# Writing down TensorE's order between attention and the gate, and exchanging two Strassen products

## The chip, the cores and the metric

One core of a Trainium2 chip runs the whole program. The metric is device microseconds of one execution; beside it stands one profiled execution, from which all rows come. TensorE multiplies matrices (its rows are marked PE, its weight loads PEld), VectorE (DVE) and ScalarE (ACT) do elementwise work and empty the accumulation banks (PSUM), GpSimd (POOL) does elementwise work on SBUF alone, and SyncE (SP) issues DMAs.

## The reference

Three stages in float32, with batch 2, 8 heads, 576 positions and head size 64, so 1152 tokens of 512 features:

```python
x = softmax_attention(mean4(q), mean4(k), mean4(v)) repeated 4x + band_attention(q, k, v)
logits = x @ w_gate                      # 512 x 8
P = exp(logits - max); 8 x: P /= rowsum; P /= colsum; P *= N / E
y = sum over 8 experts of P[:, e] * (relu(x @ w1[e]) @ w2[e])      # 512 -> 1024 -> 512
out = softplus(y @ w_in) @ w_out         # 512 -> 2048 -> 512
```

## The kernel before

**Precision.** Every float32 operand of a large product is split into a high part that TensorE takes exactly and a remainder: xh and xl for tokens, w1h and w1l for weights. A product is three matmuls (high x high, low x high, high x low) for each block of 128 rows.

**Seven products for eight.** The first layer of each expert, and of the last MLP, is computed by a Strassen-like scheme over 2 x 2 blocks: seven products (numbers 0 to 6), each of six matmuls (`product`, L589 to L601), of precomputed sums of blocks of weights and tokens (`ORDER` says in which order the tokens' seven operands are made, `operands` makes them). The tokens come in two passes, s = 0 with column halves of 256 and four tiles of 128 tokens, and s = 1 with halves of 320 and five tiles. One call of `first(n)` is step n: seven products, with a `yield` behind each. Product 4 goes into one bank of the pool m, which ScalarE copies out (t1); product 0 into a second (copied out as t5); product 5 into a third, from which VectorE makes the sum c11 = m5 + t1. Product 2 adds itself to the first bank, and ScalarE copies the sum out as u2. Product 3 adds itself to the second bank, and VectorE makes c12 = that + u2. Product 1 adds itself to the first bank, and VectorE makes c22 = that + t5. Product 6 adds itself to the first bank, which is then the fourth result. A matmul that writes a bank waits until the bank's last reader has finished. Each result goes through `hidden`: for an expert a ReLU on ScalarE (hh) and a remainder on VectorE (hl); for the last MLP a longer chain of Abs, Exp, Ln and sums.

**Second layer.** `second(n, ...)` is the share of step n in one token tile's output: six matmuls of 512 columns into a bank yps. When a group of steps is complete, `weigh` adds the bank to the accumulator on VectorE.

**Order.** Where nothing else is said, a planner decides at build time in which order each engine gets its instructions, from its own estimate of the times, earlier traced work first. Inside `tc.manual_schedule(engines={PE})` TensorE's instructions stay in the order in which the code traces them; the other engines' order is still the planner's. Before the change only the main loop (L781 on, from step 4) is written down so. There, the shares of step n, one for each token tile, are dealt among the seven products of step n + 2: with four tiles the pattern is two products, share, two, share, two, share, one, share; with five it is two, share, two, share, one, share, one, share, one, share.

**Beside attention.** Attention runs first, eight units of heads, in blocks of scores, transpositions (`turn`) and values. From half of it on, the first four steps (expert 0, first pass) are traced among its blocks by the generator `beside`: its 44 items are 4 x 7 products and 16 shares. The shares of two steps make one token tile's output, in one bank, y, which `weigh` empties before the next tile. After attention's loop the rest of `beside` is traced, then attention's buffers are given up, the second pass's operands are made in their place, then come the gate (`gates`: for each pass two groups of eight matmuls lt with 16 outputs, copied out by ScalarE as lts, and a fold by small matmuls into lg) and steps 4 and 5. TensorE's order in all this is the planner's. Then the main loop begins; it also contains the gate's normalisation (`sinkhorn`) and 32 pieces of a conversion of the last MLP's weights (`convert`, tiles cva), mostly on VectorE and GpSimd.

The banks: pool m has three, pool at has four (attention's, later the outputs'), and y is one.

Of the kernel before, what the change touches and what calls it, by code (L numbers as in the profile page):

```python
# [19 lines left out]
def attention_moe_mlp(ctx: ExitStack, tc: tile.TileContext, q, k, v, w_gate, w1, w2, w_in, w_out, out):  # L20
    nc = tc.nc
    B, H, S, D = q.shape
    NT, DM = out.shape
    E, _, FF = w1.shape
    F2 = w_out.shape[0]
    P = 128
# [15 lines left out]
    HALF = (256, 320)  # L42
# [8 lines left out]
    OPS = 7  # L51
# [12 lines left out]
    def bank(tag, name):  # L64
        return ps.tile([P, 512], F32, tag=tag, bufs={"m": 3, "y": 1, "at": 4}[tag], name=name)

    def tmp(s, name):
        return tmpp.tile([P, HALF[1]], F32, tag="t", name=name)[:, : HALF[s]]

    def pair(name):  # L70
        return pairp.tile([P, 2, 2 * HALF[1]], F32, tag="pair", name=name)
# [165 lines left out]
            yield  # L237


    ORDER = (4, 0, 5, 1, 2, 6, 3)  # L240
    FASTI = (0, 1, 2, 6)

    def halves(s, x):
        return x[:, : HALF[s]], x[:, HALF[s] : 2 * HALF[s]]
# [215 lines left out]
    nc.scalar.copy(wgs[:, :, :, :E], wg)  # L460
    nc.vector.tensor_tensor(wgs[:, :, :, E:], wg, wgs[:, :, :, :E].bitcast(F32), op=ALU.subtract)

    def gates():
        lg = bank("y", "lg")
        for s in range(2):
            lts = pair("lts").rearrange("p a c -> p (a c)")[: 2 * E]
            for j in range(2):
                lt = bank("m", "lt")
                terms = [
                    (i, w, kk, x[s]) for i, w in (((4, 1), (5, 2)), ((3, 0), (1, 1)))[j]  # L470
                    for kk in range(2) for x in (xh, xl)
                ]
                for n, (i, w, kk, x) in enumerate(terms):
                    nc.tensor.matmul(
                        lt[: 2 * E, : HALF[s]], wgs[:, w, kk, :], x[:, i, kk, :],
                        start=(n == 0), stop=(n == len(terms) - 1),
                    )
                nc.scalar.copy(halves(s, lts)[j], lt[: 2 * E, : HALF[s]])
            for t in TILES[s]:
                o = t * P - T0[s]  # L480
                nc.tensor.matmul(lg[:, t * E : (t + 1) * E], lts[:, o : o + P], fold, start=True, stop=True)
        nc.vector.tensor_reduce(m1, lg[:, : NTT * E], axis=AX.X, op=ALU.max)
        nc.vector.tensor_copy(prf, lg[:, : NTT * E])

# [45 lines left out]
    BESIDE = 4  # L530
# [45 lines left out]
    def first(n):  # L576

        e, g, s, p = steps[n]
        h = HALF[s]
        wh, wl = weights[uses[n]][0]  # L580

        if n < turned[0] and n >= BESIDE + 2 and n % 3 == 0 or n >= turned[1] and (n - turned[1]) % 3 == 0:
            hh, hl = [pairp.tile([P, 4 * HALF[1]], F32R, tag="pair", name="h3") for _ in range(2)]
        else:
            hh = hp.tile([P, 4 * HALF[1]], F32R, tag="hh", name="hh")
            hl = hp.tile([P, 4 * HALF[1]], F32R, tag="hl", name="hl")
        hh, hl = [t[:, : 4 * h].rearrange("p (f c) -> p f c", f=2) for t in (hh, hl)]

        def product(i, b=None):  # L589
            more = b is not None  # L590
            if not more:
                b = bank("m", f"m{i}")
            n = 0
            for kk in range(2):
                for x, y in ((wh, xh), (wh, xl), (wl, xh)):
                    nc.tensor.matmul(  # L596
                        b[:, :h], x[:, i, kk, :], y[s][:, i, kk, :],
                        start=(not more and n == 0), stop=(n == 5), skip_group_check=more,
                    )
                    n += 1  # L600
            return b  # L601

        def kept(name, b):
            t = tmp(s, name)
            nc.scalar.copy(t, b[:, :h])  # L605
            return t

        def combine(name, b, t):
            c = tmp(s, name)
            nc.vector.tensor_tensor(c, b[:, :h], t, op=ALU.add)  # L610
            return c

        def emit(c, f, j):
            at_ = (f, slice(j * h, (j + 1) * h))
            hidden(e, s, c, hh, hl, at_)


        b1 = product(4)
        t1 = kept("t1", b1)
        yield  # L620
        b5 = product(0)
        t5 = kept("t5", b5)
        yield

        spare[0] = product(5)
        c11 = combine("c11", spare[0], t1)
        emit(c11, 0, 0)
        yield
        product(2, b1)
        u2 = kept("u2", b1)  # L630
        yield
        product(3, b5)
        c12 = combine("c12", b5, u2)
        emit(c12, 0, 1)
        yield
        product(1, b1)
        c22 = combine("c22", b1, t5)
        emit(c22, 1, 1)
        yield
        product(6, b1)  # L640
        emit(b1[:, :h] if e < E else kept("c21", b1), 1, 0)
        ready[n] = hh, hl
        yield
# [47 lines left out]
    def lead(n):  # L691
        yield from first(n)
        f = uses[n]
        if final[f] == n and f + 3 < len(fetches):
            fetch_first(f + 3, fetches[f + 3])
# [8 lines left out]
    def beside():  # L704

        for n0 in range(0, BESIDE, 2):
            e, g, s, p = steps[n0]
            for n in (n0, n0 + 1):
                for _ in lead(n):
                    yield 6 * HALF[s]  # L710
            for i in range(len(TILES[s])):
                y = bank("y", "yps")
                for n in (n0, n0 + 1):
                    second(n, *ready[n], i, y, n == n0, n == n0 + 1)
                    if n == n0:
                        yield 6 * DM
                weigh(e, s, i, y)
                yield 6 * DM
            used(n0)
            used(n0 + 1)  # L720
# [5 lines left out]
    units[1].load()  # L726
    LAG = 2
    DENSE = 3600
    side, columns = beside(), 0
    begin = len(stream) // 2 + LAG  # L730
    for n in range(len(stream) + LAG + 1):
        if n < len(stream):
            x, blk = stream[n]
            i, j = divmod(n, len(blocks))
            x.scores(blk)
            if j == 1 and 1 <= i <= 6:
                (fetch_first if i % 2 else fetch_second)((i - 1) // 2, (i - 1) // 2)
            if j >= 2 and i + 1 < len(units):
                for g in ((0, 1), (2,))[j - 2]:
                    units[i + 1].setup(g)  # L740
                if j == 3 and i + 2 < len(units):
                    units[i + 2].load()
        for lag, what in ((LAG, "turn"), (LAG + 1, "values")):
            if 0 <= n - lag < len(stream):
                x, blk = stream[n - lag]
                getattr(x, what)(blk)
        while columns < (n - begin) * DENSE:
            columns += next(side, 1 << 30)
    for _ in side:
        pass  # L750

    CV = 12
    PIECES = 2
    ready.clear()
    at.__exit__(None, None, None)
    operand_tiles(ctx.enter_context(tc.tile_pool(name="xp1", bufs=1)), 1)
    rows.append(ctx.enter_context(tc.tile_pool(name="rows1", bufs=len(TILES[1]))))
    for kk in range(2):
        for _ in operands(1, kk, Unit.pairs[1, kk], ORDER, [nc.gpsimd]):
            pass  # L760
    gates()
    for n in (BESIDE, BESIDE + 1):
        for _ in lead(n):
            pass


    ahead = {n: [n + 2] for n in range(BESIDE, len(steps) - 2)}
# [77 lines left out]
```

## Time and profile before

| | |
|---|---|
| median of 3 runs | 1136.76 us (1133.81 to 1138.63) |
| the profiled execution | 1142.66 us, span 1140.9 us |
| mean granted TensorE clock | 0.966 |
| busy: PE, PEld, DVE, ACT, POOL | 1077.5, 943.2, 781.3, 536.3, 498.8 us |

The span is the time from the first to the last instruction. A row of the timeline gives the start, the duration, the engine with line and operation, output tile and inputs, shapes and how many rows are merged; in brackets the idle time of the engine just before it and what ended it. Durations of matmuls overlap, as a matmul's end is modelled, and starts are the surer number. A granted clock of 1.00 is 2.4 GHz, and 0.50 is 1.2 GHz.

### The profile page before, as it was taken

The page shows a single profiled execution, that of the slowest core. Times are in us where ns is not written, and L with a number is a line of the kernel's source. Part 1 is how long each engine was busy: PE and PEld are TensorE (multiplying, and loading weights), DVE is VectorE, ACT ScalarE, POOL GpSimd, SP SyncE. Part 2 cuts the span into 40 slices and gives each one's busy share as a digit, 9 for nine tenths or more (in the row PEclk, how much of TensorE's full clock was granted, in tenths as well). Part 3 has the DMA queues.
Part 4 walks back from the last instruction along what each step waited for, and adds up shares of the span by engine and source line. Part 5 has one row for each costly group of instructions (what it writes and reads, how often), then busy time and mean ns, then how long its engine had stood idle before and what let it go on. Part 6 is the DMA issues. An engine that isn't in the chain of part 4 may idle for free.

```text
span 1140.9 us, 18021 instructions
## 1 busy us (share of the span) xinstructions
PE 1077.5 (94%) x6385; PEld 943.2 (83%) x6385; DVE 781.3 (68%) x1628; ACT 536.3 (47%) x1411; POOL 498.8 (44%) x537
## 2 busy tenths in 40 slices
PE   5799998999999999998999999999999998999998
PEld 4578877899988888887888888888887887888887
DVE  6969764764677675876668476776765657766665
ACT  4657743343343344433433343343442547767763
POOL 6724144463356565556655344343553301322321
PEclk8659998999999999999999999999999998999999
DMA  8533211211143434343433323222333255154112
GB/s 174 126 88 84 61 37 38 75 34 51 49 136 111 133 97 138 101 139 102 126 111 120 111 79 126 78 94 98 119 108 114 101 204 203 60 208 170 71 38 84
DMA packets 133498, 119.71 MB, mean 105 GB/s; under 512 B 35744, under 2 KB 111776, under 8 KB 133408
## 3 DMA queue, kind: packets, MB, share of 16 engines
q1 hardware_dynamic: 133408, 118.56, 33.5%
q8 instruction: 50, 0.82, 0.3%
q14 instruction: 40, 0.33, 0.1%
HBM read 93.11 MB, written 25.43 MB: 104 GB/s over the span
## 4 chain that ended last, share of the span: by engine, by line
PE 57%; DVE 21%; DMA 7%; POOL 6%; issue 5%; ACT 3%; SPq 1%; DVEq 0%; POOLq 0%; ACTq 0%
PE yps L655 26%; PE m L596 25%; DMA raw<-in_moe_w_out 2%; POOL sums L106 2%; DMA raw<-in_moe_w_in 2%; DVE c L610 2%; DVE acc L672 2%; DVE cva L173 2%; PE sc L361 1%; DVE xl L236 1%; DVE cva L174 1%; POOL w1l L134 1%; DVE raw L180 1%; DVE cva L177 1%; DVE cva L181 1%
## 5 line engine op out<-in xcount | busy, mean ns | idle before, releaser
L596 PE MATMUL m<-xh,w1h 128*128 128x320 f32 (+1 forms) x1120 | 340.9, 304 | 34.0 <-DVE c L610 22.9
L596 PE MATMUL m<-xl,w1h 128*128 128x320 f32 (+1 forms) x1120 | 334.1, 298 | 0.0
L596 PE MATMUL m<-xh,w1l 128*128 128x320 f32 (+1 forms) x1120 | 334.0, 298 | 0.0
L596 PEld LDWEIGHTS m<-xh,w1h 128*128 128x128 f32 x1120 | 213.7, 191 | 68.1 <-DVE c L610 37.7
L596 PEld LDWEIGHTS m<-xl,w1h 128*128 128x128 f32 x1120 | 213.9, 191 | 11.8 <-DVE qkd L321 0.4
L596 PEld LDWEIGHTS m<-xh,w1l 128*128 128x128 f32 x1120 | 213.8, 191 | 0.0
L655 PE MATMUL yps<-w2h,hh 128*128 128x512 f32 x520 | 207.5, 399 | 0.3 <-DVE acc L668 0.3
L655 PE MATMUL yps<-w2l,hh 128*128 128x512 f32 x520 | 206.7, 398 | 0.0
L655 PE MATMUL yps<-w2h,hl 128*128 128x512 f32 x520 | 204.4, 393 | 0.0
L149 POOL TENSOR_TENSOR w2l<-raw,w2h 128x512 fp32r<-128x512 f32 x72 | 97.3, 1370 | 125.1 <-ACT w2h L148 125.1
L557 ACT ACTIVATE hh<-c 128x256 fp32r<-128x256 f32 (+1 forms) x138 | 60.3, 444 | 183.9 <-DVE c L610 183.4
L655 PE MATMUL yps<-w2h,h 128*128 128x512 f32 x400 | 141.4, 394 | 0.0
L134 POOL TENSOR_TENSOR w1l<-sums,w1h 128x512 fp32r<-128x512 f32 x72 | 97.0, 1361 | 95.9 <-ACT w1h L133 58.9
L570 POOL TENSOR_TENSOR ab<-ab,up 128x320 f32<-128x320 f32 (+1 forms) x64 | 54.1, 845 | 162.6 <-ACT ln L566 121.7
L610 DVE TENSOR_TENSOR c<-m,t 128x256 f32<-128x256 f32 (+1 forms) x160 | 72.3, 452 | 68.4 <-PE m L596 67.1
L672 DVE SCALAR_TENSOR_TENSOR acc<-yps,pr,acc 128x512 f32<-128x512 f32 x117 | 87.1, 744 | 45.8 <-PE yps L655 43.0
L655 PEld LDWEIGHTS yps<-w2h,hl 128*128 128x128 f32 x520 | 98.7, 190 | 23.1 <-DVE hl L558 0.4
L655 PEld LDWEIGHTS yps<-w2h,hh 128*128 128x128 f32 x520 | 99.0, 190 | 14.1 <-DVE acc L668 0.6
L558 DVE SCALAR_TENSOR_TENSOR hl<-c,hh 128x256 fp32r<-128x256 f32 (+1 forms) x138 | 85.1, 620 | 35.0 <-ACT hh L557 33.7
L655 PEld LDWEIGHTS yps<-w2l,hh 128*128 128x128 f32 x520 | 99.1, 191 | 11.7
L655 PEld LDWEIGHTS yps<-w2h,h 128*128 128x128 f32 x400 | 75.7, 189 | 13.5
L605 ACT COPY t<-m 128x256 f32<-128x256 f32 (+1 forms) x160 | 62.5, 397 | 40.9 <-PE m L596 39.4
(136 smaller groups left out, 1675.3 us busy)
## 6 DMA issues: line engine op xcount, KB each, us to landing
raw<-in_moe_w SPq DMA_DIRECT2D x72, 256.0 KB
raw<-in_moe_w SPq DMA_DIRECT2D x36, 512.0 KB
w1h<-s_in SPq DMA_DIRECT2D x10, 896.0 KB
w1l<-s_in SPq DMA_DIRECT2D x10, 896.0 KB
raw<-in_moe_w_in SPq DMA_DIRECT2D x32, 256.0 KB
raw<-in_moe_w_out SPq DMA_DIRECT2D x16, 512.0 KB
w2l<-s_out SPq DMA_DIRECT2D x10, 512.0 KB
w2h<-s_out SPq DMA_DIRECT2D x10, 512.0 KB
```

The costliest lines, as they stand in the source:

```text
L106: nc.gpsimd.tensor_tensor(sums[i], a, b, op=op)
L134: nc.gpsimd.tensor_tensor(lo[:, part], sums, hi[:, part].bitcast(F32), op=ALU.subtract)
L149: nc.gpsimd.tensor_tensor(lo[:, i], raw[:, i], hi[:, i].bitcast(F32), op=ALU.subtract)
L173: nc.vector.tensor_scalar(a, high, 0x07FFFFFF, 3, op0=ALU.bitwise_and, op1=ALU.logical_shift_left)
L557: nc.scalar.activation(hh, c, AF.Relu)
L558: nc.vector.scalar_tensor_tensor(out=hl, in0=c, scalar=0.0, in1=hh.bitcast(F32), op0=ALU.max, op1=ALU.subtract)
L570: nc.gpsimd.tensor_tensor(ab, ab, up, op=ALU.subtract)
L596: nc.tensor.matmul(b[:, :h], x[:, i, kk, :], y[s][:, i, kk, :], start=(not more and n == 0), stop=(n == 5), skip_group_check=more,)
L605: nc.scalar.copy(t, b[:, :h])
L610: nc.vector.tensor_tensor(c, b[:, :h], t, op=ALU.add)
L655: nc.tensor.matmul(y, a[:, f, tok], b[:, f, :], start=(start and m == 0), stop=(stop and m == 5))
L672: nc.vector.scalar_tensor_tensor(out=acc[t], in0=y, scalar=pr[:, t, e : e + 1], in1=acc[t], op0=ALU.mult, op1=ALU.add,)
```

## The change

Products 1 and 3 change places in `first`, and operands 3 and 6 in `ORDER`. The gate becomes a generator in six parts, takes its banks from the pool at and its result tiles from the pool of temporaries, and keeps the two results of a pass in tiles of their own, so that one tile of the second pass is folded in two pieces. The rest of `beside` (14 items after the loop over attention), the gate's parts and the products of steps 4 and 5 are traced in a written-down order: six products of step 3 with the first pass's three gate parts between, four shares, then the 14 products of steps 4 and 5, with one item behind every second of them: three shares, three gate parts, one share.

```diff
-    ORDER = (4, 0, 5, 1, 2, 6, 3)
+    ORDER = (4, 0, 5, 1, 2, 3, 6)
...
-    def gates():
-        lg = bank("y", "lg")
+    def gates(banks):
+
+        lg = bank("at", "lg")
         for s in range(2):
-            lts = pair("lts").rearrange("p a c -> p (a c)")[: 2 * E]
+            lts = [tmp(1, "lts")[: 2 * E] for _ in range(2)]
             for j in range(2):
-                lt = bank("m", "lt")
+                if s or not j:
+                    whole = bank(banks, "lt")
+                lt = whole if s else halves(s, whole)[j]
...
-                nc.scalar.copy(halves(s, lts)[j], lt[: 2 * E, : HALF[s]])
+                nc.scalar.copy(lts[j][:, : HALF[s]], lt[: 2 * E, : HALF[s]])
+                yield
             for t in TILES[s]:
                 o = t * P - T0[s]
-                nc.tensor.matmul(lg[:, t * E : (t + 1) * E], lts[:, o : o + P], fold, start=True, stop=True)
+                for j in range(2):
+
+                    a, b = max(o, j * HALF[s]), min(o + P, (j + 1) * HALF[s])
+                    if a < b:
+                        nc.tensor.matmul(
+                            lg[a - o : b - o, t * E : (t + 1) * E], lts[j][:, a - j * HALF[s] : b - j * HALF[s]],
+                            fold, start=True, stop=True,
+                        )
+            yield
...
+        product(1, b1)
+        c22 = combine("c22", b1, t5)
+        emit(c22, 1, 1)
+        yield
         product(3, b5)
         c12 = combine("c12", b5, u2)
         emit(c12, 0, 1)
-        yield
-        product(1, b1)
-        c22 = combine("c22", b1, t5)
-        emit(c22, 1, 1)
         yield
         product(6, b1)
...
-    side, columns = beside(), 0
+    side, columns, shares = beside(), 0, BESIDE * (OPS + len(TILES[0]))
...
-            columns += next(side, 1 << 30)
-    for _ in side:
-        pass
+            columns += next(side)
+            shares -= 1
...
-    gates()
-    for n in (BESIDE, BESIDE + 1):
-        for _ in lead(n):
-            pass
+
+    gate = gates("at")
+    with tc.manual_schedule(engines={mybir.EngineType.PE}):
+        for n in range(shares - 4):
+            next(side)
+            if n in (1, 3, 5):
+                next(gate)
+        among = iter((side, side, side, gate, gate, gate, side))
+        for m, _ in enumerate(x for n in (BESIDE, BESIDE + 1) for x in lead(n)):
+            if m % 2:
+                next(next(among))
+        for x in (side, gate):
+            for _ in x:
+                pass
```

## Rows read from the trace of the kernel before

**Rows 1.** The page's first part: engine, busy us, share of span, instructions.
```profile
PE 1077.5 (94%) x6385; PEld 943.2 (83%) x6385; DVE 781.3 (68%) x1628; ACT 536.3 (47%) x1411; POOL 498.8 (44%) x537
```

**Rows 2.** TensorE's waits, 230 us to the end: us in total, times, longest.
```profile
PE m L596 <- DVE c L610: 22.1, 27, 2.3
PE m L596 <- ACT u L605: 3.7, 5, 2.2
```

**Rows 3.** The timeline of TensorE in the main loop: start us, us, instruction, idle before.
```profile
346.63 0.30 PE L596 MATMUL m<-xh,w1h 128*128 128x320 f32 x1
...
510.76 0.31 PE L596 MATMUL m<-xh,w1l 128*128 128x320 f32 x1
...
515.25 0.41 PE L596 MATMUL m<-xh,w1h 128*128 128x320 f32 x1 [1.91 <-DVE c L610]
...
1118.44 0.40 PE L655 MATMUL yps<-w2h,h 128*128 128x512 f32 x1
...
1119.83 0.28 PE L596 MATMUL m<-xh,w1h 128*128 128x256 f32 x1
```

**Rows 4.** The timeline of VectorE around step 31.
```profile
508.17 1.51 DVE L173 TENSOR_SCALAR cva<-raw 128x512 uint32<-128x512 uint32 x1 [3.70 <-POOL w1l L134]
...
514.31 0.48 DVE L610 TENSOR_TENSOR c<-m,u 128x320 f32<-128x320 f32 x1
```

**Rows 5.** The timeline of ScalarE in the main loop.
```profile
347.42 0.41 ACT L605 COPY u<-m 128x320 f32<-128x320 f32 x1
...
508.85 0.43 ACT L605 COPY u<-m 128x320 f32<-128x320 f32 x1 [0.98 <-PE m L596]
...
512.43 0.47 ACT L557 ACTIVATE hh<-c 128x320 fp32r<-128x320 f32 x1 [3.16 <-DVE c L610]
...
1119.88 0.35 ACT L605 COPY u<-m 128x256 f32<-128x256 f32 x1
```

**Rows 6.** Lines L558 and L610: duration in ns, shortest/median/longest, first and last start.
```profile
L558 DVE SCALAR_TENSOR_TENSOR hl<-c,hh x138: 403/482/1546, 95.3 to 927.8; 128x256 fp32r<-128x256 f32 x72, 128x320 fp32r<-128x320 f32 x66
L610 DVE TENSOR_TENSOR c<-m,t x160: 395/449/493, 92.8 to 1123.3; 128x256 f32<-128x256 f32 x80, 128x320 f32<-128x320 f32 x80
```

**Rows 7.** The timeline of TensorE from attention's end to the main loop.
```profile
133.47 0.29 PE L596 MATMUL m<-xh,w1h 128*128 128x256 f32 x1
...
147.54 0.28 PE L474 MATMUL lt<-xh,wgs 128*16 128x256 f32 x1
...
151.38 0.28 PE L596 MATMUL m<-xl,w1h 128*128 128x256 f32 x1
151.50 0.28 PE L596 MATMUL m<-xh,w1l 128*128 128x256 f32 x1
...
155.47 0.50 PE L655 MATMUL yps<-w2h,hh 128*128 128x512 f32 x1 [0.28 <-DVE acc L668]
...
160.46 0.32 PE L474 MATMUL lt<-xl,wgs 128*16 128x320 f32 x1 [1.55 <-DVE xl L236]
...
164.85 0.32 PE L474 MATMUL lt<-xh,wgs 128*16 128x320 f32 x1 [0.61 <-ACT lts L478]
...
173.27 2.17 PE L481 MATMUL lg<-fold,lts 16*128 16x8 f32 x18
...
182.95 0.42 PE L596 MATMUL m<-xh,w1h 128*128 128x320 f32 x1 [0.50 <-DVE hl L558]
...
189.53 0.42 PE L596 MATMUL m<-xh,w1h 128*128 128x320 f32 x1 [2.25 <-DVE hl L558]
```

**Rows 8.** Busy us in three stretches (instructions), then granted clock, DMA share, GB/s.
```profile
30.00:60.00 30.00, 21.75 (x167) 16.49 (x166) 29.49 (x73) 20.11 (x82) 23.19 (x26) 0.67 0.53 122
175.00:180.00 5.00, 5.00 (x25) 4.98 (x26) 1.35 (x4) 1.33 (x3) 0.00 (x0) 0.68 0.00 0
190.00:195.00 5.00, 4.63 (x19) 3.45 (x18) 0.28 (x1) 0.42 (x1) 4.20 (x6) 0.66 0.35 105
```

More of the change, by code (lines that the diff above doesn't have):

```diff
@@ L747, in attention_moe_mlp @@
         while columns < (n - begin) * DENSE:
-            columns += next(side, 1 << 30)
-    for _ in side:
-        pass
+            columns += next(side)
+            shares -= 1
     CV = 12
     PIECES = 2
-    ready.clear()
     at.__exit__(None, None, None)
@@ L760, in attention_moe_mlp @@
             pass
-    gates()
-    for n in (BESIDE, BESIDE + 1):
-        for _ in lead(n):
-            pass
+    gate = gates("at")
[11 more added lines that the diff above has]
+                pass
+    for n in range(BESIDE):
+        del ready[n]
     ahead = {n: [n + 2] for n in range(BESIDE, len(steps) - 2)}
```

## The prediction

> **What bounds the kernel now.** I read the page first: TensorE is busy for 94% of the span, VectorE for 68% [rows 1]. So the end moves only with TensorE's own work, its clock, and the stretches in which it waits. The second view is the list of TensorE's waits from 230 us to the end, where its order is already written down. It has two large entries [rows 2]: 22.1 us in 27 waits for a VectorE sum (L610), and 3.7 us in 5 waits for a ScalarE copy named u (L605). In the timeline, counted off against the written order of blocks, each of the 27 stands in front of a product 6 and each of the 5 in front of a product 1. Product 6 writes the bank that holds product 1 until the sum c22 has read it; product 1 writes the bank that the copy u2 has to read first.
>
> A wait costs more than its idle time. A share's matmul lasts 0.40 us in its row while six of them take 1.39 us, 0.23 each, so 0.16 us of the wait hides under the end of the row before; and the first matmul after a wait lasts 0.41 instead of 0.30 us [rows 3]. With 0.26 us added to each, the waits for sums cost 22.1 + 27 x 0.26 = 29.1 us and those for copies 3.7 + 5 x 0.26 = 5.0 us, together 34.1 us.
>
> Why a sum is late is seen at 515.25 [rows 3, 4]: VectorE stood 3.70 us in front of the first instruction of a conversion piece, because GpSimd still read a buffer; the accumulations and sums behind it then came late in a row, c12 at 514.31 and c22 right after it. ScalarE had made u2 at 508.85, ahead of a ReLU for which it then waited 3.16 us [rows 5].
>
> **Products 1 and 3 exchanged.** No instruction is added or removed; six matmuls change places with six. Between product 1 and product 6 now lies one share; afterwards product 3 lies there too (0.71 us at 256 columns, 0.88 at 320), and a second share when five shares are dealt to seven products. In exchange, product 1 follows product 2 with one share between, where product 3 runs now.
>
> The sum c22 will take the place on VectorE that c12 has now, right behind the product that precedes it. So I took the lateness of today's c12 behind product 3 as that of c22, and set it against the new cover (2.1 us for four shares and 320 columns, 3.3 for five and 256). In seven steps it is still too late, the worst being step 31: product 3's last matmul starts at 510.76 and ends at 511.07, c12 ends at 514.79, 3.7 us later, so 1.7 us of the wait stay [rows 3, 4]. The seven sum to 5.7 us, with 0.1 for each first matmul 6.4. The other waits of product 6 are hidden by product 3.
>
> Then the new wait. Product 1 would start where product 3 starts today, if u2 were done. Of the 74 copies from step 6 on, 23 end later. The first is at 347.42, ending 1.2 us after product 3 began at 346.63; the last is at 1119.88, ending 0.4 us after 1119.83 [rows 3, 5]. The 23 sum to 18.5 us, 8.7 of them in seven steps of the experts and 9.8 in sixteen of the last layer, where ScalarE has Abs, Exp and Ln of the previous sum ahead of the copy. With 0.1 each, 20.8 us. Queued behind a waiting product 1 is all of TensorE; what waits behind u2 on ScalarE is the ReLU of the next sum, which nobody needs before the shares two steps on.
>
> The bounds: the new waits are zero if u2 always goes ahead, as in step 31, and larger by 24.9 us in 18 steps if it always stands behind a late ReLU. I take the copies where the trace has them. The exchange is then 6.4 + 20.8 - 34.1 = **-6.9 us**.
>
> One rule speaks against even that. The longest VectorE instruction that reads two SBUF tiles in this group lasted 1546 ns against a median of 482, while the sums, which read one tile and PSUM, stayed between 395 and 493 [rows 6]. The Trainium skill, "SBUF — State Buffer", section "Who interferes with whom", says that a VectorE instruction with two SBUF inputs and a GpSimd instruction that reads SBUF exclude each other, and one with at most one SBUF input does not contend. By that rule, with which these rows agree, the lateness is made by GpSimd's work ahead of the sums, and an exchange on TensorE leaves it as it is; the rival "the wait moves" below is that case.
>
> **From attention to gate.** Before, the planner mixes this work; afterwards its place on TensorE is fixed behind attention. What goes [rows 7, 8]:
> - Gate products wait at 160.46 and 164.85 for the second pass's operands and the copy of a gate result: 1.55 + 0.61 + 2 x 0.26 = 2.7 us. Afterwards six products, the first pass's gate and four shares lie ahead of the first need of these operands, over 12 us of work.
> - The fold's 18 short rows at 173.27 come in one run of 2.17 us, and from 175 to 180 the granted clock is 0.68, partly the level of 1.2 GHz: 5.0 x 0.32 = 1.6 us. In two pieces between products this should go.
> - The wait at 182.95: 0.50 + 0.26 = 0.8 us, covered by a gate product (eight matmuls at 0.15).
> - The wait at 189.53: 2.25 + 0.26 = 2.5 us; one share (1.39) now lies in front, so 1.4 goes.
> - After it the clock was 0.66 from 190 to 195 [rows 8]; of 4.63 x 0.34 = 1.6 us I take half, 0.8.
>
> Together 7.3 us. What comes: before, the six products left of step 3 (36 matmuls from 133.47 to 151.50, 0.12 apart), 16 gate matmuls (from 147.54, 1.9 us) and two shares (2.8 us) ran in gaps of attention's end [rows 7]. These 9.0 us are now traced behind it. Attention's own chain of scores, exponential, transposition and values ends earlier without them by somewhere between nothing and all of it; no row shows how much, so I take half: 4.5 us. Two token tiles in a row on the only y bank wait for the accumulation between them, like 155.47: 0.28 + 0.26 = 0.5 us. Two more fold rows are 0.2 us. With fewer matmuls in attention's last 5 us the clock can fall as it did from 30 to 60 us, to 0.67 [rows 8]: 0 to 1.7 us, I take 0.8. Sum 6.0, net **-1.3 us**. From both sides: -6.6 (the order lets the work fill gaps as before) to +6.5 (nothing given back and no clock gained). No DMA changes its place in a queue: the four steps' later uses of second weights issue none. The operands' order 3 before 6 exchanges two conversions of like length and is worth nothing. The gate's banks and result tiles change pools (m and y for at, pair for tmp); of the waits in rows 7 only the one at 164.85 hangs on them, counted above, so I price that at nothing; if attention still holds all four at banks when the gate comes, it is part of the +6.5.
>
> **The sum.** -6.9 - 1.3 = -8.2 us. The profiled execution took 1142.66 us, 1.76 beyond its span, and would come to 1134.5. It lies 5.9 us above the median of 1136.76, so on the median's scale the forecast is **1128.6 us**, 0.7% faster.
>
> **Rivals.**
> - *The copy goes ahead.* The planner puts u2 before a late ReLU in half of the cases. For it: it does so in step 31. Against: the last layer's copies stand behind Ln. Half of 20.8 goes: 1118 us.
> - *The wait moves.* VectorE's lateness passes from product 6 to whatever needs it next, all 34.1 us of it, and the exchange gives nothing. For it: rows 4 and 6. Against: today's waits stand in front of product 6 alone, whose cover is shortest. 1136.76 - 1.3 = 1135.5 us.
> - *The written order holds attention's fill back.* Nothing of the 9.0 us is given back and the clock falls: +6.5 - 6.9, 1136.4 us.
> - *The written order doesn't hold.* The products still fill attention's gaps: -6.6 - 6.9, 1123 us.
> - *Slower: the copy stuck behind a late ReLU.* In 18 steps of the experts u2 is now made before c11 is there; if the new order puts the ReLU first, product 1 waits for VectorE, ReLU and copy in turn: +24.9 us and 18 x 0.1, while the 6.4 us of product 6 vanish. 1128.6 + 20.3 = 1149 us; it decides from about half of these steps on.
>
> **How the numbers follow.** Forecast 0.36 (own range 1124 to 1134), copy ahead 0.18, wait moves 0.16, fill held back 0.12, order doesn't hold 0.08, copy stuck 0.10. A measurement of this kernel tells about 0.5% from no change, so faster is below 1131.1 and slower above 1142.4. Faster: 0.26 of the forecast's, 0.17, 0.07 and 0.02 each of the two middle ones, 0.54. Slower: 0.08 of the stuck copy and 0.04 of the tails, 0.12. The rest, 0.34, is no change. The range runs from 1115, beyond the copy ahead, to 1142, where half of the stuck copies would lie.
>
> **What would show it.** In the waits from 230 us on, those for sums should fall from 22.1 to some 5 us, now with few cases, and those for u rise from 3.7 to about 15. If both are small, the copy goes ahead; if sums stay above 15, the wait moves; if u exceeds 25, it is stuck. Between 155 and 195 us, waits on xl and the fold's single run should be gone and the clock near 1.00; if attention's last values matmul is not earlier than 153 us, the fill is lost. The forecast is wrong if the waits in the steps change by less than 3 us, or if the first written-down block after the gate starts later than at 187 us.

## The result and the profile after

The changed kernel takes 1148.33 us (median of 4 runs, 1144.83 to 1157.04) beside 1135.28 us of the kernel before (4 runs, 1133.0 to 1138.63): a ratio of 1.0109 [1.007, 1.0148]. It is 1.1% slower, where the forecast was 1128.6 us and the range ended at 1142. Its profiled execution took 1150.44 us (span 1148.6), against 1142.66 us before.

The page's first part and, below it, the row of line L608, a product's first matmul (busy, mean ns, idle before):

```profile
PE 1073.5 (93%) x6387; PEld 940.8 (82%) x6387; DVE 780.2 (68%) x1628; ACT 531.4 (46%) x1411; POOL 499.7 (44%) x537
...
L608 PE MATMUL m<-xh,w1h 128*128 128x320 f32 (+1 forms) x1120 | 340.8, 304 | 43.4 <-ACT u L617 24.4
```

Against [rows 1] nothing was added: TensorE is busy 4 us less in a span that is 7.7 us longer. TensorE's waits from 230 us to the end (us in total, times, longest), which answer to [rows 2]:

```profile
PE m L608 <- ACT u L617: 21.2, 16, 3.0
PE m L608 <- DVE h L570: 5.2, 5, 1.4
PE m L608 <- DVE c L622: 4.0, 7, 0.9
PE m L608 <- DVE hl L570: 3.6, 3, 1.4
```

Waits for sums fell from 22.1 to 4.0 us, waits for copies rose from 3.7 to 21.2. What was not foreseen is h and hl, both the remainder behind a ReLU (h in the steps that use a third buffer): 2.8 us in 5 waits before, 8.8 in 8 now. Together 34.0 us against 28.6.

To see where the time is, I cut the profiled executions at the same work: the 169th matmul of attention's values (L423), attention's last one, the main loop's first share, and the first share of the last layer's loop (step 62). The columns "start", "to attention's end", "to main loop", "experts" and "last layer" are the times between these points, in us. The clock column is worked out from the granted clock: (1 - clock) x time, summed over the two stretches between the 169th matmul and the main loop; idle is time in which no matmul row runs there. The two overlap where TensorE waits at a low clock, by 1 us in after. Numbers in brackets are the experiments below.

```
                             start    to attention's  to main  idle  clock  experts  last
                             to 169th  end            loop                           layer
before                        106.5        48.6         35.4     6.2    1.8   730.5   219.8
after                         100.9        44.5         51.1    10.5   12.0   727.7   224.6
exchange alone (1)             96.1        47.3         33.2     5.1    0.0   728.5   225.0
order alone (2)                98.9        45.1         51.7    14.9    8.0   734.0   220.4
exchange in experts (3)       101.3        47.2         33.2     5.0    0.0   727.5   219.8
operands later (4)            105.4        43.4         44.2     8.5    5.2   729.7   225.9
rest planned (5)               99.4        46.3         33.8     4.8    0.0   728.0   224.5
more beside attention (6)     103.1        47.6         38.1     8.1    1.7   728.4   224.8
more pushed (7)               100.1        37.8         54.4    10.9    6.2   729.2   225.4
experts, rest planned (11)     97.9        45.9         34.6     3.6    1.7   727.1   218.9
kept busy (8)                  99.3        47.8         48.8    10.4    3.2   730.4   226.1
filled late (8)                99.2        42.9         51.2    11.9    8.5   732.4   226.7
share first (9)                97.4        44.5         44.6     7.5    8.5   727.9   224.5
share and operands (10)       100.0        44.9         40.5     6.6    5.1   727.7   224.5
```

From the 169th matmul to the main loop, after needs 95.5 us where before needs 84.0 (+11.5); the experts gain 2.8, the last layer loses 4.8. TensorE's work there is the same in all rows: less idle and clock, each has 73 to 76 us left (83 in kept busy, which has 7.1 us of work added), so the differences lie in these two columns. The first column, 5.6 us shorter, goes with the moment from which the clock stays at 1.00 (about 85 us in before, 70 in after); over the rows it varies by 10 us, and no kernel is judged by it. Before's profiled execution lies some 7 us above its median, and so does the one of experiment 4, so differences of 2 or 3 us against its row are not worth much, and the ratios decide.

The timeline of TensorE in that stretch, the rows that answer to [rows 7]:

```profile
131.97 0.49 PE L402 MATMUL tp<-ident,ex 128*72 128x128 f32 x3
...
136.14 0.80 PE L361 MATMUL sc<-kT,fine 128*128 128x72 f32 x6
138.96 0.83 PE L402 MATMUL tp<-ident,ex 128*72 128x128 f32 x3 [2.01 <-DVE ex L382]
...
143.72 1.60 PE L423 MATMUL pv<-et,vw 72*64 72x64 f32 x24
145.25 0.40 PE L477 MATMUL lt<-xh,wgs 128*16 128x256 f32 x1
...
150.52 0.39 PE L608 MATMUL m<-xh,w1h 128*128 128x256 f32 x1 [2.10 <-ACT u L617]
...
154.94 0.58 PE L608 MATMUL m<-xh,w1h 128*128 128x256 f32 x1 [1.02 <-DVE c L622]
...
163.95 0.50 PE L667 MATMUL yps<-w2h,hh 128*128 128x512 f32 x1 [0.78 <-DVE acc L680]
...
184.79 1.36 PE L489 MATMUL lg<-fold,lts 16*128 16x8 f32 x12
...
190.64 0.39 PE L667 MATMUL yps<-w2h,hl 128*128 128x512 f32 x1
...
195.40 0.41 PE L608 MATMUL m<-xh,w1h 128*128 128x320 f32 x1 [3.48 <-DVE hl L570]
196.38 0.61 PE L667 MATMUL yps<-w2h,hh 128*128 128x512 f32 x1
```

From 136.95 on attention has nothing ready (its exponentials ex are late), and no other matmul runs; before, shares and products ran between attention's blocks. The same three transpositions take 0.49 us ahead of the wait and 0.83 behind it.

The written-down order has a part in that. It puts the gate's first part behind two of the six products of step 3 and in front of the other four, and the gate's first matmul (145.25) came only behind attention's last (143.72, merged). So it was in all seven experiments with this order (2, 4, 7, 8 twice, 9, 10): just the two products ahead of the gate's first part ran beside attention. Before, the gate's first matmul ran at 147.54 [rows 7], ahead of attention's last:

```profile
154.61 0.57 PE L423 MATMUL pv<-et,vw 72*64 72x64 f32 x12
```

The gate's banks now come from the pool at, which attention uses up to its end. That this is what holds the gate's part, and the four products with it, is likely but not shown: no run has the old banks with the new order. The windows (busy us of PE, PEld, DVE, ACT, POOL, then granted clock, DMA share, GB/s) show how long the low clock lasts; they answer to [rows 8]:

```profile
135.00:140.00 5.00, 2.99 (x31) 2.26 (x31) 4.96 (x12) 3.09 (x17) 4.47 (x5) 0.84 0.62 185
140.00:145.00 5.00, 4.64 (x49) 3.25 (x48) 3.07 (x7) 2.37 (x10) 1.76 (x3) 0.50 0.08 25
145.00:150.00 5.00, 3.42 (x20) 2.52 (x18) 4.03 (x8) 4.12 (x12) 2.90 (x3) 0.64 0.01 3
150.00:155.00 5.00, 3.46 (x21) 2.96 (x21) 5.00 (x10) 1.83 (x6) 2.04 (x2) 0.70 0.00 0
155.00:160.00 5.00, 5.00 (x18) 4.46 (x19) 1.89 (x5) 1.38 (x4) 0.00 (x0) 0.50 0.00 0
160.00:165.00 5.00, 4.22 (x14) 3.00 (x14) 0.69 (x1) 0.00 (x0) 0.00 (x0) 0.77 0.00 0
...
185.00:190.00 5.00, 5.00 (x27) 4.85 (x27) 1.51 (x5) 0.62 (x2) 0.00 (x0) 0.66 0.00 0
190.00:195.00 5.00, 1.92 (x11) 1.48 (x9) 4.86 (x7) 3.07 (x8) 4.10 (x4) 1.00 0.28 105
195.00:200.00 5.00, 4.22 (x15) 3.02 (x16) 0.63 (x2) 0.43 (x1) 1.95 (x3) 0.66 0.00 0
```

For most of 25 us TensorE runs at 1.2 GHz or waits. The wait at 150.52 is explained by ScalarE: the copy u that product 1 needs stands behind eleven casts of the second pass's operands (L235) and one of the gate's copies:

```profile
145.88 0.46 ACT L235 CAST xh<-xf 128x320 fp32r<-128x320 f32 x1 [1.52 <-DVE xf L438]
...
149.75 0.45 ACT L235 CAST xh<-xf 128x320 fp32r<-128x320 f32 x1
150.11 0.36 ACT L617 COPY u<-m 128x256 f32<-128x256 f32 x1
...
189.38 0.93 ACT L127 CAST w1h<-raw 128x256 fp32r<-128x256 f32 x2 [5.71 <-PE m L608]
...
191.25 1.18 ACT L569 ACTIVATE hh<-c 128x320 fp32r<-128x320 f32 x3
```

VectorE has the same queue: its sum for 154.94 stands behind thirteen remainders (L236). The last two rows belong to the wait at 195.40; experiment 9 is about them.

### The profile page after: what moved, and what is told of

Its sections match the earlier page's. It is cut to its first block, busy times and chain, and to the rows that moved or that the text cites. A ratio compares the mean times of both kernels' runs of the same rounds, so it can differ in the third digit from the quotient of the medians.

```text
span 1148.6 us, 17989 instructions
## 1 busy us (share of the span) xinstructions
PE 1073.5 (93%) x6387; PEld 940.8 (82%) x6387; DVE 780.2 (68%) x1628; ACT 531.4 (46%) x1411; POOL 499.7 (44%) x537
## 4 chain that ended last, share of the span: by engine, by line
PE 48%; DVE 24%; POOL 9%; DMA 7%; issue 6%; ACT 5%; SPq 1%; POOLq 0%; DVEq 0%; ACTq 0%
PE yps L667 23%; PE m L608 21%; POOL sums L106 3%; DVE acc L684 2%; DMA raw<-in_moe_w_in 2%; DVE cva L173 2%; DMA raw<-in_moe_w 2%; DVE c L622 2%; DVE xl L236 2%; POOL w2l L149 2%; DVE w1l L128 2%; DVE hl L570 2%; POOL w1l L134 1%; DVE cva L174 1%; POOL cva L191 1%
## 5 line engine op out<-in xcount | busy, mean ns | idle before, releaser
L608 PE MATMUL m<-xh,w1h 128*128 128x320 f32 (+1 forms) x1120 | 340.8, 304 | 43.4 <-ACT u L617 24.4
L608 PE MATMUL m<-xl,w1h 128*128 128x320 f32 (+1 forms) x1120 | 334.1, 298 | 0.0
L608 PE MATMUL m<-xh,w1l 128*128 128x320 f32 (+1 forms) x1120 | 334.1, 298 | 0.0
L608 PEld LDWEIGHTS m<-xh,w1h 128*128 128x128 f32 x1120 | 213.9, 191 | 77.0 <-ACT u L617 36.3
L608 PEld LDWEIGHTS m<-xl,w1h 128*128 128x128 f32 x1120 | 214.2, 191 | 11.4 <-DVE xl L236 0.3
L608 PEld LDWEIGHTS m<-xh,w1l 128*128 128x128 f32 x1120 | 214.0, 191 | 0.0
L570 DVE SCALAR_TENSOR_TENSOR hl<-c,hh 128x256 fp32r<-128x256 f32 (+1 forms) x138 | 87.9, 643 | 32.9 <-ACT hh L569 31.6
L106 POOL TENSOR_TENSOR sums<-raw 128x256 f32<-128x256 f32 x72 | 58.8, 835 | 54.1 <-DMA raw<-in_moe_w 41.7
```

What stands on the lines that cost most here:

```text
L106: nc.gpsimd.tensor_tensor(sums[i], a, b, op=op)
L570: nc.vector.scalar_tensor_tensor(out=hl, in0=c, scalar=0.0, in1=hh.bitcast(F32), op0=ALU.max, op1=ALU.subtract)
L608: nc.tensor.matmul(b[:, :h], x[:, i, kk, :], y[s][:, i, kk, :], start=(not more and n == 0), stop=(n == 5), skip_group_check=more,)
```

## The experiments

Each was timed against the kernel before. In the expectations, theory A puts the loss on the written-down order from attention to the gate, and not on the exchange.

**1. The exchange alone.** Before, with products 1 and 3 (and operands 3 and 6) exchanged and no other edit.

```diff
-    ORDER = (4, 0, 5, 1, 2, 6, 3)
+    ORDER = (4, 0, 5, 1, 2, 3, 6)
...
+        product(1, b1)
+        c22 = combine("c22", b1, t5)
...
         product(3, b5)
         c12 = combine("c12", b5, u2)
```

> The kernel before with only products 1 and 3 (and operands 3 and 6) exchanged; the order from attention to the gate stays the planner's. Theory A (the written-down order costs the time; in the main loop the exchange only passes waits on, by the two traces -2.7 us in the experts and +4.6 in the last layer): about +2 us on the kernel before, 1137 +- 3 us; waits of TensorE from 230 us on: sums about 4 us, copies u about 21 us, remainders hl and h about 9 us. Rival B (the exchange costs the 13 us): 1147 us or more. Rival C (my prediction for this part): -6.9 us, 1128 us.

1134.65 us, 0.9976 [0.9949, 1.0004]: no loss, where 2 us more than before were expected. Its waits from 230 us on are those of after:

```profile
PE m L596 <- ACT u L605: 20.1, 14, 3.0
PE m L596 <- DVE h L558: 5.1, 5, 1.4
PE m L596 <- DVE c L610: 4.9, 5, 1.8
PE m L596 <- DVE hl L558: 3.6, 3, 1.4
```

By the table it gains 2.0 us in the experts and loses 5.2 in the last layer, so from the main loop on it is 3.2 us slower; it gains 3.5 between the 169th matmul and the main loop, where the low clock of before is missing too. The exchange does not make the kernel slower; it brings 2.7 us where the forecast had 6.9, and with this interval that is not told from nothing.

**2. The order alone.** After, with products 1 and 3 and the operands put back.

```diff
-        product(1, b1)
-        c22 = combine("c22", b1, t5)
...
+        product(1, b1)
+        c22 = combine("c22", b1, t5)
```

> The changed kernel with products 1 and 3 and operands 3 and 6 put back; only the written-down order from attention to the gate is left. Theory A: about +11 us, 1146 us; TensorE's clock at 0.50 for much of 139 to 162 us, copies and sums waiting behind the second pass's operands; waits from 230 us on as before (sums 22, copies 4 us). Rival B: within 3 us of the kernel before. Rival C (the sum of my prediction for this part): -1.3 us.

1151.09 us, 1.0112 [1.0073, 1.0152]. The whole loss is here, without the exchange. On top of the exchange the order costs more still: after's 1.0109 against 0.9976 in experiment 1 is 1.3%, or 15 us, and by the table 95.5 us stand against 80.5.

**3. The exchange in the experts only**, before's order elsewhere (operands 3 and 6 are exchanged for all).

```diff
+        for i in (1, 3) if e < E else (3, 1):
+            if i == 1:
+                product(1, b1)
...
+                product(3, b5)
```

> The kernel before with products 1 and 3 exchanged in the eight experts only; the last layer keeps 3 before 1 (operands 3 and 6 are exchanged for all). Theory A: the last layer's +4.6 us go, so -2.7 us on the kernel before, 1133 us, and 4.6 below the exchange alone; copies u wait about 12 us from 230 us on, none of it long after 950 us. If lateness just moves, also in the last layer, it equals the exchange alone.

1131.43 us, 0.9922 [0.9892, 0.9953]: by the ratio 9 us faster than before (by the medians 7), more than expected, and 3.2 below experiment 1. The table puts 3.0 us of it in the experts and 3.6 between the 169th matmul and the main loop. The waits from 230 us on:

```profile
PE m L596 <- ACT u L605: 12.7, 7, 3.0
PE m L596 <- DVE c L610: 8.5, 13, 1.5
PE m L596 <- DVE h L558: 5.2, 5, 1.4
```

The last layer is back at 219.8 us: the loss there was product 1 behind a copy that stands behind Abs, Exp and Ln, as these rows of after show for one of its eight waits there:

```profile
1087.49 0.46 ACT L576 ACTIVATE ab<-ab 128x320 f32<-128x320 f32 x1
1087.99 0.47 ACT L578 ACTIVATE ln<-ab 128x320 f32<-128x320 f32 x1
1088.36 0.41 ACT L617 COPY u<-m 128x320 f32<-128x320 f32 x1
...
1088.82 0.41 PE L608 MATMUL m<-xh,w1h 128*128 128x320 f32 x1 [1.45 <-ACT u L617]
```

**4. The second pass's operands later.** After, with the operands traced behind step 3's products, the first gate and the first shares.

```diff
-    for kk in range(2):
-        for _ in operands(1, kk, Unit.pairs[1, kk], ORDER, [nc.gpsimd]):
-            pass
...
                 next(gate)
+        for kk in range(2):
+            for _ in operands(1, kk, Unit.pairs[1, kk], ORDER, [nc.gpsimd]):
+                pass
```

> The changed kernel with one thing moved: the second pass's operands are traced after step 3's products, the first pass's gate and the first shares, instead of before them, so that the planner gives these products' copies and sums precedence on ScalarE and VectorE. If the waits of 2.1 us (copy u behind twelve conversions) and 1.0 us (sum behind the remainders) and the clock that falls with them make up the loss: 4 to 7 us faster than the changed kernel, 1142 us. If the loss is made by attention's end having no other products beside it (clock already 0.50 from 139 us on), less than 2 us faster; the later operands may then be waited for by step 4's first product.

1143.3 us, 1.0052 [1.0026, 1.0078], about 0.6% better than after, as expected if these queues matter. The wait for u falls from 2.10 to 0.46 us:

```profile
152.39 0.39 PE L608 MATMUL m<-xh,w1h 128*128 128x256 f32 x1 [0.46 <-ACT u L617]
```

**5. The rest planned.** After, with the first expert's remaining items left to the planner, as before; only the gate's parts stay between the products of steps 4 and 5. Experiments 5, 6, 7 and 11 share a theory P (items pushed behind attention cost, by queues and clock) and its rival G (the gate's order costs).

```diff
+    for _ in side:
+        pass
...
-        for n in range(shares - 4):
-            next(side)
-            if n in (1, 3, 5):
-                next(gate)
-        among = iter((side, side, side, gate, gate, gate, side))
+        among = iter((gate, gate, gate, gate, gate, gate, gate))
...
-                next(next(among))
+                next(next(among), None)
```

> After's exchange in every step, and of its written-down order only the gate's parts between the first fourteen products of steps 4 and 5; the rest of the first expert's items is left to the planner among attention, as before. Theory P (the order costs because items are pushed behind attention, where they meet copies and sums queued behind the second-pass operands and a clock of 1.2 GHz): the 12.5 us go, ratio 0.996 to 1.001 of before (1134 to 1139 us, where the exchange alone gave 0.9976). Theory G (what costs is the gate's order among the products of steps 4 and 5): it stays above 1.006 (over 1145 us).

1134.14 us, 0.9968 [0.9948, 0.9988]. The loss is gone, and the gate's parts among the products of steps 4 and 5 cost nothing that shows; G falls. But the run takes away two things at once, the pushed items and the gate's first part in front of four products, and doesn't tell them apart. The same stretch as above in its windows, at 2.4 GHz throughout:

```profile
140.00:145.00 5.00, 4.22 (x48) 3.15 (x48) 4.32 (x10) 3.12 (x13) 4.72 (x6) 1.00 0.13 38
145.00:150.00 5.00, 4.25 (x29) 3.27 (x28) 4.16 (x7) 3.70 (x11) 2.72 (x3) 1.00 0.00 0
150.00:155.00 5.00, 4.05 (x21) 3.52 (x22) 5.00 (x10) 1.99 (x6) 2.01 (x3) 1.00 0.00 0
```

**6. More beside attention, and 7. more pushed.** After with DENSE, the pace of the filling, raised or lowered: 8 or 22 items are traced behind attention instead of 14.

```diff
-    DENSE = 3600
+    DENSE = 4224
...
-            if n in (1, 3, 5):
+            if n in (1, 2, 3):
```

> After with 36 instead of 30 or so of the 44 items of the first expert put out among attention: only eight shares (11 us at 2.4 GHz) stay behind it, with the gate's parts between them. Theory P: with fewer products behind attention that need copies and sums, most of the loss goes: 1137 to 1142 us (ratio 0.999 to 1.003). Theory G: as after, 1.009 to 1.013. A rival inside P, that any item left behind costs its whole time: about 1144.

1141.93 us, 1.0034 [1.0009, 1.0059], just above P's range and far from G's. Only shares are left here, so no product of step 3 stands behind the gate's first part. For the other run DENSE is 2880 and the gate's places are after's.

> After with eight more products of the first expert held back until attention is over (22 items behind it instead of 14 to 16; the eight are about 5.7 us at 2.4 GHz and 11 us at 1.2 GHz). Theory P: slower than after by 4 to 8 us, 1152 to 1158 us (ratio 1.014 to 1.018). Theory G: the same as after within 2 us, as the gate's order is unchanged.

1148.65 us, 1.0097 [1.0068, 1.0126]: as after. P's price by the item falls. Attention's end came 6.7 us sooner without the eight products, and the stretch behind it grew by 3.3. What costs is not moved work by the piece but the waits and the clock that come with it, here 17.1 us of both, in after 22.5. Here too just two products ran ahead of the gate's first part.

**8. Kept busy.** Sixty matmuls that nobody reads, among attention's last tiles of after. C says that the loss begins where TensorE runs dry there, W that it lies behind attention.

```diff
+        for _ in range(2 if n >= len(stream) - 2 else 0):
+            b = bank("at", "idle")
+            for m in range(6):
+                nc.tensor.matmul(b[:, :256], now[0][:, 0, 0, :], xh[0][:, 0, 0, :256], start=(m == 0), stop=(m == 5))
```

> After with sixty extra matmuls of 256 columns (7.1 us at 2.4 GHz, results read by nobody) put among the last tiles of attention; everything else stands. In after's profile the stretch from attention's values to the main loop lost 12.0 us to the 1.2 GHz clock and 10.5 us to idle. Theory C (the loss begins where TensorE runs out of work in attention's last tiles, and the clock then falls): the added work fills waits of some 2 us and keeps the clock at 2.4 GHz, clock loss down to 5 us or less, so 0 to 4 us faster than after although more is computed (1144 to 1148 us, ratio 1.006 to 1.010). Theory W (the clock falls for the waits behind attention, on copies queued behind second-pass operands, whatever is done before): clock loss stays over 9 us, and the added work makes it 4 to 7 us slower than after (ratio 1.014 to 1.018).

1153.82 us, 1.0128 [1.0088, 1.0169], between the two. Windows:

```profile
145.00:150.00 5.00, 5.00 (x51) 4.62 (x49) 2.48 (x5) 2.38 (x8) 3.53 (x5) 1.00 0.36 104
150.00:155.00 5.00, 3.07 (x24) 2.50 (x23) 5.00 (x8) 3.23 (x11) 3.07 (x4) 1.00 0.00 0
155.00:160.00 5.00, 3.18 (x18) 2.83 (x18) 3.70 (x10) 1.74 (x5) 0.00 (x0) 0.88 0.00 0
```

The added work keeps the clock at 1.00 through attention's end, and the clock's loss falls from 12.0 to 3.2 us, as C said; but the waits behind the operands remain (idle 10.4 us against 10.5), as W said. Its 7.1 us of added work is about what the clock gave back (8.8).

The other run of this pair puts out the same items three tiles later and denser:

```diff
-    DENSE = 3600
+    DENSE = 4480
...
-        while columns < (n - begin) * DENSE:
+        while columns < (n - begin - 3) * DENSE:
```

> After with the same thirty items of the first expert put out during attention, but beginning three of its tiles later and denser, so that the last tiles have as much beside them as in the kernel before; as many items stay behind attention, in the same written-down order. Theory C: the last tiles' waits are covered, the clock holds, 3 to 8 us faster than after (ratio 1.002 to 1.008). Theory W, or the count of pushed items decides: as after, 1.009 to 1.013.

1154.14 us, 1.0111 [1.0062, 1.0159]. No gain: the waits on ex stay (2.5 us in two), the windows go down to 0.50 from 140 to 145. Being traced later did not make the planner place the items there, so this run decides little.

**9. The last share first.** What ends the ReLUs' wait at 191.25 above? The pool for hidden units has two buffers, so step 5 writes the one that step 3's shares read; the last of these is written down behind step 5's products and ends at 191.03. One place in the list is changed:

```diff
-        among = iter((side, side, side, gate, gate, gate, side))
+        among = iter((side, side, side, side, gate, gate, gate))
```

> After with one item moved: the first expert's last share is written down before the gate's parts instead of behind the last product of step 5. In after that share ends at 191.0 us, and only then do step 5's four ReLUs run (191.25 on ScalarE), although the first of their sums was there at 181.7: the hidden units of step 5 take the buffer that this share reads. Theory B (buffer): ReLUs run as their sums come, the wait of 3.5 us before the main loop falls to 1.5 us or less and the clock of 0.66 behind it (1.7 us) goes: 3 to 6 us faster than after, ratio 1.005 to 1.008. Rival: the wait is set by ScalarE's casts of the next weights or by VectorE's queue, and stays: 1.009 to 1.013.

1144.97 us, 1.0046 [1.0024, 1.0067]: B holds, with a gain just over its range. ReLUs run singly as their sums come, from 175.57 on, and the wait before the main loop is

```profile
185.44 0.42 PE L608 MATMUL m<-xh,w1h 128*128 128x320 f32 x1 [1.48 <-DVE hl L570]
```

with the clock at 1.00 in the windows from 185 us on.

**10. Share and operands together** (experiments 4 and 9 in one kernel).

> The second pass's operands brought out later (measured 1.0052) and the share moved as in the other run, together. If the two are separate parts of what the written-down order costs: 3 to 5 us below the operands later alone, ratio 1.001 to 1.003, wait before the main loop 1.5 us or less. If they are the same loss seen twice: 1.004 to 1.008.

1139.9 us, 1.0011 [0.9986, 1.0037]. The two are separate losses: together they bring 1.0%, singly 0.6% each. Of the 1.3% that the order costs on top of the exchange, 0.35% is left, and there the windows still show 0.50 from 140 to 145, where attention runs dry and the gate's first part still stands behind its end.

**11. The version that is faster.** The exchange in the experts (3) with the rest planned (5).

> The exchange in the experts' steps alone (measured 0.9922 of before by itself) with the filling of the first expert left to the planner as in the run with the rest planned. Theory P: 0.989 to 0.994 of before (1126 to 1132 us), as good as the exchange in the experts alone or a little better for the gate's copies covered by the products of steps 4 and 5. Theory G: 4 us or more slower than the exchange in the experts alone, over 0.996.

1127.1 us, 0.992 [0.9889, 0.9952]: faster than both kernels. It is not told apart from experiment 3 by its ratio, so what the gate's order adds to the exchange is not shown.

## Why the prediction was wrong

*The step that failed* is "From attention to gate", -1.3 us where the runs show about +12: the order alone costs 1.12%, and 84.0 us become 96.7 with it and 95.5 in after.

- "Together 7.3 us" should go. In after they went only in name: the operands' wait on TensorE went, but 10.5 us of other idle time stand in place of 6.2, and the clock costs 12.0 us in place of 1.8. The exchange alone, with the planner's order, has no clock loss and 5.1 us idle, and its single run of 18 fold rows (161.47) is followed by a clock of 1.00: the clock's 2.4 of the 7.3 us did not hang on the planner's order. Whether it is the exchange or the execution that spares them is not shown, with one profile of each kernel.
- The flaw is in "lie ahead of the first need of these operands, over 12 us of work". I counted TensorE's work ahead of the gate, and not what that work needs in its turn: copies and sums, queued on ScalarE and VectorE behind the same operands' casts and remainders. Experiment 4 prices that at about 0.6%.
- The gate's change of pools: "I price that at nothing". The gate's first part came behind attention's end, and four products stood behind it, as shown above. What this costs by itself no run shows; it is still so in experiment 10, with the 0.35% that are left.
- "one share (1.39) now lies in front, so 1.4 goes" of the 2.25 us at 189.53. That share reads the buffer which the awaited ReLUs write; it lengthened the wait to 3.48 us, and the clock fell to 0.66 behind it. Experiment 9 prices it at about 0.6%. Within it, VectorE's three remainders took 3.20 us, 1.07 each against 0.49 to 0.69 in experiment 9, while GpSimd ran a remainder of weights:

```profile
190.90 2.76 POOL L134 TENSOR_TENSOR w1l<-sums,w1h 128x512 fp32r<-128x512 f32 x2 [6.65 <-ACT w1h L133]
...
191.75 3.20 DVE L570 SCALAR_TENSOR_TENSOR hl<-c,hh 128x320 fp32r<-128x320 f32 x3
```

The Trainium skill, "SBUF — State Buffer", section "Who interferes with whom", says that a VectorE instruction with two SBUF inputs and GpSimd's reading exclude each other. These rows agree.

- "In two pieces between products this should go": the second piece, twelve rows at 184.79, is followed by a granted clock of 0.66 from 185 to 190 us, as the single run was before. Nothing went.
- "I take half: 4.5" came out, but in part by luck: attention from its 169th matmul to its end took 44.5 us instead of 48.6, 4.1 given back, though 3.5 us of the clock's loss lie in these 44.5 and two of the six products still ran there.
- "0 to 1.7 us, I take 0.8" for the clock was the term sized worst. I had a row for a long low clock (30 to 60 us, [rows 8]) and bounded the loss by one window of 5 us. (The wait on the y bank, 0.78 us at 163.95, was forecast at 0.5.) The low clock began between 138 and 139 us and lasted, with one rise from 149 to 152, to about 162; waits of 2.01, 2.10 and 1.02 us lie in that time.

*The exchange* was -6.9. Alone it brought 2.7 us (experiment 1), but not where I had them. Split by stage, which I did not do, my terms were 15.8 - 27.0 = -11.2 us in the experts and 11.4 - 7.2 = +4.2 in the last layer; the table has -2.0 and -3.0 in the experts (experiments 1 and 3) and +5.2 in the last layer (experiment 1). The last layer's term stood, the experts' did not (the 9 us of experiment 3 are of the whole kernel, and only 3.0 of them lie in that stretch). Sums wait 4.0 us in 7 places, copies 21.2 in 16, 9.1 of them in the last layer (forecast 9.8). With the prediction's 0.26 for each wait sums cost 5.8 (forecast 6.4) and copies 25.4 (forecast 20.8). No term at all had the waits for h and hl, which grew by 6.0 us. What failed is "the other waits of product 6 are hidden by product 3": hidden they are, but the next step's product 5 then waits: it takes the bank that product 6's remainder on VectorE has to read first. In seven of the eight waits this remainder stands behind weight remainders (L128) and an accumulation:

```profile
626.01 2.66 DVE L128 TENSOR_TENSOR w1l<-raw,w1h 128x256 fp32r<-128x256 f32 x2
628.59 0.74 DVE L684 SCALAR_TENSOR_TENSOR acc<-yps,pr,acc 128x512 f32<-128x512 f32 x1
629.25 0.47 DVE L570 SCALAR_TENSOR_TENSOR h<-m,h 128x320 fp32r<-128x320 f32 x1
...
629.78 0.38 PE L608 MATMUL m<-xh,w1h 128*128 128x256 f32 x1 [1.38 <-DVE h L570]
```

The waits from 230 us on did not shrink, then (28.6 us before, 33.7 with the exchange alone): the rival "the wait moves" describes the main loop better than the forecast does.

*The rivals.* The time is that of "copy stuck behind a late ReLU" (1149), but its mechanism did not happen: u costs 21.2 us, not 46. "The fill held back" named the right place and gave it +6.5, its upper bound, which was too low by half; the bound had the pushed work in it but none of the new waits, and it still took off 4.9 us of old ones. That is also why the range missed.

*The signs named in advance* pointed to this: the main loop began at 196.4 us, later than the 187 that was to show the forecast wrong, and the clock between 155 and 195 was not near 1.00 (0.50 from 155 to 160, 0.66 from 185 to 190). One sign misled: attention's last values matmul, which was to lie at 153 us or later if the fill was lost, ended by 145.3, and the time was lost behind it.

What stays open: whether the gate's banks are what holds the four products back and so thins out the filling in attention's end (in after TensorE waits 2.01 us there, in the run with the rest planned 0.8); and whether that is the last 0.35% of experiment 10.

## What to carry to other kernels

When an order is written down for one engine, the others keep theirs: for every item moved, follow what it reads and which buffer it frees, and look for both in the other engines' queues. Here a share written down too late held a buffer, a gate part that came late had four products behind it, and work that "covers" a wait waited on the same queues. In a stretch where the engine is just busy enough, price a wait with the low clock that follows it, over the whole stretch until the waits end; a filler that looks free to move may be what keeps the clock. And sum an edit by stage: the same exchange gained 2 to 3 us in the experts and lost some 5 in the last layer, and was best made in the experts alone.

## What the runs showed of the hardware

- The clock can cost more than the waits: 10.2 us more of it in after than before (12.0 against 1.8), beside 4.3 us more of idle time. TensorE had waited ahead of the long fall (2.99 us busy of 135 to 140) and of the one behind 195 us (1.92 of 190 to 195); the one from 186 us on followed a wait of 0.57 us and the short rows of the fold. But 3.62 us busy of 150 to 155 in experiment 6 and 3.63 of 145 to 150 in experiment 11 were followed by 1.00.
- Sixty matmuls without a reader kept the granted clock at 1.00 up to about 159 us and cost about 2 us of their 7.1 in the end (1.0128 against 1.0109, with intervals that overlap).
- These kernels reach attention's 169th matmul between 96.1 and 106.5 us. The latest two (106.5 and 105.4) have the clock at 1.00 for good only from about 84 us on, the earliest (96.1) from about 61; with one profile of each kernel, chance and plan are not told apart.
